# A planned linear-attention and feed-forward kernel: the order of units drawn anew, unread totals dropped, the last two copies in separate buffers

## Chip, cores and metric

The kernel runs on one core of a Trainium2 chip. The metric is device time in microseconds of one execution, the median of several. Before the change it is 183.63 us (four runs, 182.86 to 183.89).

## What is computed

Inputs are `q`, `k`, `v` and `f_logit`, each of shape (4 batches, 8 heads, 768 steps, 48), and two weights. A recurrent attention with a forget gate per key dimension comes first; its output, 3072 rows of 384, goes through a feed-forward block with exact GELU. All inputs and the output are float32.

```python
f = 1.0 / (1.0 + np.exp(-f_logit))
for t in range(S):
    state = f[:, :, t, :, None] * state + einsum('bhd,bhe->bhde', k[:, :, t], v[:, :, t])
    y[:, :, t] = einsum('bhd,bhde->bhe', q[:, :, t], state)
x = y.transpose(0, 2, 1, 3).reshape(3072, 384)
h = x @ w_in                                   # 384 -> 2048
out = (0.5 * h * (1 + erf(h / sqrt(2)))) @ w_out   # 2048 -> 384
```

## The kernel before, in words

**Chunks and units.** The 768 steps of a batch are cut into 6 chunks of 128, so there are 24 chunks n = 0..23, and two neighbouring chunks make a unit u = 0..11 (chunks 2u and 2u+1). Units 0 to 4 (`PAIRS`) hold their 256 steps interleaved ("pair" units, function `attn_pair`); units 5 to 11 hold the chunks one after the other (`attn_nat`). A unit is also a group g = u of the feed-forward block (`ffn_group`).

**Steps of a unit**, by the names that the plan gives them:

- `E`, `L` (ScalarE, L478 and L481): exponential and logarithm of the gate logits, in the table of exponentials.
- `C` (TensorE, L494 to L504): running sums of the log gates within a chunk, by a matmul with a triangle. Beside them, 4 small matmuls (8 for a pair unit, in its second half) compute the chunk's totals, into the same PSUM bank.
- `RG`, `GT`, `GL` (ScalarE, L509 to L518): exponentials of the negative sums, the sums and the totals.
- `KP`, `QP` (VectorE, L524): the keys and queries times these. `VC` (L529): the values in bf16, mostly on GpSimd.
- Transposes of both: by TensorE (`Tk`, `Tq`, L557) and a copy (`KQ`), or from unit 4 on by a DMA transpose (`KD`, L545).
- `S` (TensorE, L684 or L745): the chunk's addition to the state. `R` (VectorE) and `T`, `SB` (GpSimd) carry the state on with the totals `gl`. Chunk 5 of each batch needs none of this, since no chunk follows it.
- `A` (TensorE, L661 or L723) and `AM` (VectorE, L570): scores and their mask; `Y` (or `YI`, `YX`): the output; `YB`: its copy in bf16.
- `XT` and `X`, or from unit 5 on the DMA transpose `XD` (L618): the output transposed, as the input of the feed-forward block.
- `F1` (TensorE, L801): 8 steps of 6 matmuls to a group, each into one PSUM bank; `GE` (ScalarE, L811): GELU of each, in the table of GELU; `F2` (L820): for each chunk 4 steps of 4 matmuls, all into one bank; `O` (L834, for the last chunk L827): the copy to SBUF; `st`: the store.

`F1.8.5` is step 5 of group 8, `F2.17.2` step 2 of chunk 17.

**The planner.** `Plan.add` records every step with an estimated duration, what it reads and writes, its buffers and a priority. `Plan.run` places the steps one at a time, by its own estimate of time, and among those that can start in the same twentieth of a microsecond it takes the one with the lowest priority number. The order in which steps are placed is the order in which each engine's instructions are emitted, and it also decides which buffer a step gets. On the chip each engine then works through its list in order and waits at a step until what it needs is there. Before placing, each priority gets random amounts: a first one for all steps from one seed, and a second one from the generator of the step's unit (`SEEDS`, one seed per unit), whose width depends on the seed:

```python
if SEEDS[k]:
    w = (0.5, 1.0, 3.0, 8.0)[SEEDS[k] % 4]
    o.prio += own[k].uniform(-w, w)
```

When a step of ScalarE needs the other table than the last one, a table load is emitted ahead of it (L865).

**PSUM.** Of 8 banks 4 (`s_fh`) serve F1 and F2 (and the first units), 4 (`s_m`) the attention.

**Loads.** `LOADS` is the list of loads in order: `f3` is the gate logits of unit 3, `u4` all four inputs of unit 4, `i` and `o` pieces of the two weights, which GpSimd's queue loads. SyncE's queue issues all other loads, the stores and the DMA transposes, in one order. Where the list changes from one queue to the other, a load waits until an earlier weight has landed.

**Warm-up.** In the first 30 us, where the plan leaves TensorE idle, matmuls on a tile `junk` are put in (L859).

Of the kernel before, what the change touches and what calls it, by code (L numbers as in the profile page):

```python
# [9 lines left out]
F32 = mybir.dt.float32  # L10
BF16 = mybir.dt.bfloat16
AF = mybir.ActivationFunctionType
ALU = mybir.AluOpType
# [11 lines left out]

SPREAD, SEED = (1.0, 97)

SEEDS = [0, 684, 383, 3363, 2427, 131, 74, 3619, 3555, 1021, 519, 3174]

EAGER = 0.0  # L30

# [50 lines left out]
class Plan:  # L82
# [30 lines left out]
    def run(self):  # L113
# [4 lines left out]
        for o in self.ops:  # L118
            if o.prio > -5:
                k = min(max(int(o.prio % 1000) // 20, 0), len(SEEDS) - 1)  # L120
                o.prio += rng.uniform(-SPREAD, SPREAD)
                if SEEDS[k]:
                    w = (0.5, 1.0, 3.0, 8.0)[SEEDS[k] % 4]
                    o.prio += own[k].uniform(-w, w)
        act, switched, mode = None, 0.0, 0
        port = {"DVE": (0.0, 0.0), "POOL": (0.0, 0.0)}
        for o in self.ops:
# [75 lines left out]

SIZES = [2, 2, 2, 2, 2, 2, 2, 2, 2, 2, 2, 2]
PAIRS = [0, 1, 2, 3, 4]
WIN = [1024, 512, 512]
# [13 lines left out]
KDMA = [4, 5, 6, 7, 8, 9, 10, 11]  # L222
AJ = [2, 3, 4, 5, 6, 7, 8, 10, 11]
NGT = 4
WARM = 30.0
LOADS = ['f0', 'k0', 'v0', 'q0', 'f1', 'v1', 'k1', 'q1', 'i0', 'k2', 'f2', 'v2', 'q2', 'i1', 'i2', 'i3', 'o0', 'o1', 'o3', 'f3', 'o2', 'k3', 'q3', 'u4', 'v3']
LOADS += [f"u{n}" for n in range(12) if f"u{n}" not in LOADS and f"c{2 * n}" not in LOADS and f"f{n}" not in LOADS]


@with_exitstack  # L230
def kernel(
# [29 lines left out]
    def slots(n, shape, dt, name):  # L261
        return Slots(n, [one.tile(shape, dt, name=f"{name}{i}") for i in range(n)])
# [21 lines left out]
    s_vb = slots(10, [C, HD], BF16, "vb")  # L284
    s_gt, s_rg = slots(3, [C, HD], F32, "gt"), slots(3, [C, HD], F32, "rg")
    s_gl = slots(6, [C, 2, P2], F32, "gl")
    s_kq = slots(3, [C, 2, P2, 2, C], BF16, "kq")
    s_am = slots(8, [C, P2, C], BF16, "am")
    s_rr, s_tn = slots(3, [C, P2, 2 * D], F32, "rr"), slots(3, [C, P2, 2 * D], F32, "tn")
# [51 lines left out]
    for i in range(3):  # L341
        P.add("DVE", 0.2, lambda i=i: nc.vector.memset(
            s_sb.tiles[i].rearrange("p a b -> p (a b)").bitcast(F32), 0.0), wr=[f"sbz{i}"], prio=-70)
    z_lf = [f"lfz{i}" for i in range(3)]
    z_sc = [f"scz{i}" for i in range(NQ)]
    z_sb = [f"sbz{i}" for i in range(3)]
# [104 lines left out]
    def decays(u):  # L451
# [16 lines left out]
        for a, b, lo, hi in parts:  # L468
# [7 lines left out]
            def expop(lo=lo, hi=hi):  # L476
# [4 lines left out]
            P.add("ACT", d, lambda view=view, lo=lo, hi=hi: nc.scalar.activation(lf.t()[:, :, lo:hi, 0:D], view(), AF.Ln, bias=1.0),  # L481
                  rd=[("e", u, i) for i in range(a, b + 1)] + z_lf, wr=[("lf", u, i) for i in range(a, b + 1)],
                  bufs=[fl, lf], table="exp", prio=pr, name=f"L{u}")
        gps = [(s_fh if u in EG else s_m).new() for _ in range(2)]
        for j, n in enumerate(ns):
            y = X[n]
            gt, rg = s_gt.new(), s_rg.new()
            y.update(sc=s_sc.new(), vb=s_vb.new())
            pr = 20 * u + 10 * j

            def cum(j=j, g=gps[j]):
                g = g.t()
                if not pair:
                    nc.tensor.matmul(g[:, 0:HD], trin, lf.t()[:, j, :, 0:D], start=True, stop=True)  # L494
                    for p in range(P2):
                        nc.tensor.matmul(g[:, HD + p:HD + p + 1], lf.t()[:, j, 2 * p:2 * p + 2, :], negcol,  # L496
                                         start=True, stop=True, skip_group_check=True)
                    return
                nc.tensor.matmul(g[:, 0:HD], trip[:, 0, :], lf.t()[:, 0, :, 0:D], start=True, stop=False)
                nc.tensor.matmul(g[:, 0:HD], trip[:, 1 - j, :], lf.t()[:, 1, :, 0:D], start=False, stop=True)  # L500
                if j:
                    for i in range(2):
                        for p in range(P2):
                            nc.tensor.matmul(g[:, HD + 2 * p:HD + 2 * p + 2], lf.t()[:, i, 2 * p:2 * p + 2, :], negp,  # L504
                                             start=False, stop=(i == 1), skip_group_check=True)
            P.add("PE", (0.54 if j else 0.33) if pair else 0.27, cum,
                  rd=([("lf", u, 0), ("lf", u, 1), "trip", "negp"] if pair else [("lf", u, j), "trin", "negcol"]), wr=[("g", n)],
                  bufs=[lf, gps[j], gt, rg, y["sc"], gl], prio=pr, opens=gps[j], name=f"C{n}")
            P.add("ACT", 0.40, lambda g=gps[j], rg=rg: nc.scalar.activation(rg.t(), g.t()[:, 0:HD], AF.Exp, scale=-1.0),  # L509
                  rd=[("g", n)], wr=[("rg", n)], bufs=[gps[j], rg], table="exp", prio=pr, name=f"RG{n}")  # L510
            P.add("ACT", 0.40, lambda g=gps[j], gt=gt: nc.scalar.activation(gt.t(), g.t()[:, 0:HD], AF.Exp),  # L511
                  rd=[("g", n)], wr=[("gt", n)], bufs=[gps[j], gt], table="exp", prio=pr + 1, name=f"GT{n}")
            if not pair:
                P.add("ACT", 0.19, lambda g=gps[j], j=j: nc.scalar.activation(
                    gl.t()[:, j, :], g.t()[:, HD:HD + P2], AF.Exp),
                    rd=[("g", n)], wr=[("gl", n)], bufs=[gl, gps[j]], table="exp", prio=pr + 2, name=f"GL{n}")
            elif j:
                P.add("ACT", 0.19, lambda g=gps[j]: nc.scalar.activation(  # L518
                    gl.t(), g.t()[:, HD:HD + 2 * P2].rearrange("a (p c) -> a c p", c=2), AF.Exp),
                    rd=[("g", n)], wr=[("gl", n - 1), ("gl", n)], bufs=[gl, gps[j]], table="exp", prio=pr + 2,  # L520
                    name=f"GL{n}")
            for w, nm, a, b, off in ((0, "kp", "kt", rg, 0), (1, "qp", "qt", gt, 1)):
                pl = n in (GKP, GQP)[w]
                P.add("POOL" if pl else "DVE", 0.80 if pl else 0.475, lambda w=w, a=a, b=b, y=y, j=j, pl=pl: (nc.gpsimd if pl else nc.vector).tensor_tensor(  # L524
                    y["sc"].t()[:, w, :, 0:D], half(u, x[a], j), b.t().rearrange("p (h d) -> p h d", h=H), ALU.mult),
                    rd=[("gt" if w else "rg", n), (a, n)] + z_sc, wr=[(nm, n)], bufs=[y["sc"], x[a], b], prio=pr + off,
                    port=True, name=f"{nm.upper()}{n}")
            hv = u in HVC
            P.add("ACT" if hv else "POOL", 0.40 if hv else 0.47, lambda y=y, j=j, hv=hv: (nc.scalar.copy if hv else nc.gpsimd.tensor_copy)(  # L529
                y["vb"].t().rearrange("p (h d) -> p h d", h=H), half(u, x["vt"], j)),  # L530
                rd=[("vt", n)], wr=[("vb", n)], bufs=[y["vb"], x["vt"]], prio=pr, name=f"VC{n}")
# [173 lines left out]
    def attn_pair(u):  # L705
# [52 lines left out]
        def intra():  # L758
            for hh in range(2):
                for p in range(P2):  # L760
                    h = 2 * p + hh
                    for jk in range(2):
                        for cc in range(2):
# [2 lines left out]
                                             vbs[jk].t()[r, D * h:D * h + D], start=(h == 0 and jk == 0),  # L766
                                             stop=(cc == 0 and osb is None and hh == 1 and p == P2 - 1 and jk == 1),
                                             skip_group_check=True)
        P.add("PE", 0.5, intra, mode=1, rd=[("am", u, a, b) for a in range(2) for b in range(2)] + [("vb", n) for n in ns],
              wr=[("yi", n) for n in ns] + ([("yp", n0)] if osb is None else []), bufs=yps + vbs + sum(ams, []) + [U[u]["yb"]],  # L770
              prio=pr + PRI["Y"], opens=yps[0], name=f"YI{u}")
        for cc, n in enumerate(ns):
            o = (osb, mid)[cc]
            if o is None:
                continue
            P.add("PE", 0.2, lambda cc=cc, o=o: interp(yps[cc], kq, cc, o),
                  mode=1, rd=[("yi", n), ("sb", n - 1, 0), ("sb", n - 1, 1)] + [("kq", m) for m in ns], wr=[("yp", n)],
                  bufs=[yps[cc], kq, o], prio=pr + PRI["Y"] + 10 * cc, name=f"YX{n}")
# [3 lines left out]
    def ffn_group(g):  # L782
# [31 lines left out]
        for s_ in range(s):  # L814
            op, osb = s_fh.new(), s_os.new()
            n = first[g] + s_
            for r in range(4):
                def f2(s_=s_, r=r, op=op):
                    for fo in range(4 * r, 4 * r + 4):
# [2 lines left out]
                P.add("PE", 0.65, f2, rd=[("gT", g, fo // pk) for fo in range(4 * r, 4 * r + 4)] + [f"wout{r}"],  # L822
                      wr=[("o", n)], bufs=[op, gT], prio=pr + PRI["F"] + s_, held=True, name=f"F2.{n}.{r}")
            if n == NCH - 1:
                for i, eng in enumerate(("ACT", "DVE")):
                    h = slice(i * d_model // 2, (i + 1) * d_model // 2)
                    P.add(eng, 0.27, lambda h=h, i=i, op=op, osb=osb: copier(not i)(osb.t()[:, h], op.t()[:, h]),  # L827
                          rd=[("o", n)], wr=[("os", n, i)], bufs=[op, osb], prio=pr - 1000, name=f"O{n}")
                    P.add("DMA", 0.3, lambda h=h, i=i, n=n, osb=osb: (nc.sync if i else nc.scalar).dma_start(
                        out=out[n * C:(n + 1) * C, h], in_=osb.t()[:, h]), rd=[("os", n, i)], bufs=[osb], prio=-5, lag=4.0,  # L830
                        name=f"st{n}")
                continue
            od = n in ODVE
            P.add("DVE" if od else "ACT", 0.475 if od else 0.40, lambda op=op, osb=osb, od=od: copier(not od)(osb.t(), op.t()[:, 0:d_model]),  # L834
                  rd=[("o", n)], wr=[("os", n)], bufs=[op, osb], prio=pr - 1000, name=f"O{n}")
            P.add("DMA", 0.6, lambda n=n, osb=osb: nc.sync.dma_start(out=out[n * C:(n + 1) * C, :], in_=osb.t()),
                  rd=[("os", n)], bufs=[osb], prio=-5, lag=4.0, name=f"st{n}")

    g = 0
    for u in range(NU):  # L840
# [58 lines left out]
```

## Time and profile before

| | before |
|---|---|
| median of 4 runs | 183.63 us (182.86 to 183.89) |
| the profiled execution: its time | 183.65 us |
| its span in the profile | 181.5 us |
| busy: TensorE, ScalarE, VectorE, GpSimd | 172.4, 126.3, 95.2, 52.6 us |
| table loads of ScalarE at L865 | 15, 1283 ns each |
| granted TensorE clock | full |

The profile is of one execution; its time is 2.15 us more than its span. "Busy" is the time in which at least one instruction of the engine was under way; matmuls overlap, so a busy TensorE can still have waited within a step. In the profile's names `ps` is any PSUM bank, `sc` the products KP and QP, `lf` the log gates, `gl` the exponentials of the totals, `osb` the tile from which an output is stored.

### The profile page before, as it was taken

The numbers are of one execution on the slowest core, as the hardware profiler recorded it, in microseconds if no ns is written. First come the engines' busy times: TensorE is split into PE (matmuls) and PEld (weight loads), VectorE is DVE, ScalarE is ACT, GpSimd is POOL, SyncE is SP. The second block draws the span as 40 slices with busy tenths as digits, with TensorE's granted clock in tenths as the row PEclk, the third lists the DMA queues.
The fourth block names the chain that finished last, engine by engine and source line by source line (L and its number), as shares of the span: only waits on it lengthen the run. The fifth ranks groups of instructions, "written<-read, shape, count | busy, mean of one in ns | idle before, by whom it ended". The sixth has DMA issues, their size and how long they took to land.

```text
span 181.5 us, 4908 instructions
## 1 busy us (share of the span) xinstructions
PE 172.4 (95%) x1991; PEld 131.7 (73%) x1991; DVE 95.2 (52%) x185; ACT 126.3 (70%) x215; POOL 52.6 (29%) x116
## 2 busy tenths in 40 slices
PE   7689799999999999999999999999999999999992
PEld 2356479866778977669679689966696966887960
DVE  4289730068888650689277770627785217171020
ACT  2775098982986899989957689787483697360900
POOL 7757860003224810150352014014353112100000
PEclk9999999999999999999999999999999999999999
DMA  5999999999999999999999989989999973702112
GB/s 143 261 261 230 262 182 209 205 230 271 273 191 223 173 209 182 203 170 207 204 203 217 171 165 233 179 167 152 215 222 125 202 134 84 208 4 43 43 51 79
DMA packets 106933, 32.61 MB, mean 180 GB/s; under 512 B 102048, under 2 KB 106016, under 8 KB 106912
## 3 DMA queue, kind: packets, MB, share of 16 engines
q1 hardware_dynamic: 104992, 29.07, 76.8%
q0 software_dynamic: 1776, 3.15, 9.7%
q8 instruction: 15, 0.25, 0.6%
q10 hardware_dynamic: 144, 0.10, 0.2%
q14 instruction: 6, 0.05, 0.1%
HBM read 25.17 MB, written 4.72 MB: 165 GB/s over the span
## 4 chain that ended last, share of the span: by engine, by line
PE 79%; DMA 8%; SPq 6%; ACT 2%; DVE 2%; issue 1%; DVEq 0%; ACTq 0%
PE ps L801 33%; PE ps L820 32%; DMA fl<-in_f_logit_dram 6%; SPq L433 6%; DMA xT<-yb 2%; PE ps L661 2%; PE ps L697 2%; PE ps L494 1%; PE ps L638 1%; PE ps L684 1%; PE ps L723 1%; PE ps L557 1%; PE ps L765 1%; PE ps L745 1%; PE ps L644 1%
## 5 line engine op out<-in xcount | busy, mean ns | idle before, releaser
L811 ACT ACTIVATE gT<-ps 128x512 bf16<-128x512 f32 x96 | 58.5, 668 | 23.3 <-PE ps L801 21.7
L801 PE MATMUL ps<-xT,win 128*128 128x256 bf16 x576 | 68.6, 273 | 1.1 <-DMA win<-in_moe_w_in_dram 0.8
L820 PE MATMUL ps<-wout,gT 128*128 128x384 bf16 x384 | 68.3, 326 | 0.0
L801 PEld LDWEIGHTS <-win 128*128 128x128 bf16 x576 | 61.3, 114 | 3.6 <-DMA win<-in_moe_w_in_dram 1.1
L820 PEld LDWEIGHTS <-gT 128*128 128x128 bf16 x384 | 35.8, 98 | 20.9
L524 DVE TENSOR_TENSOR sc<-kt,rg 128x384 bf16<-128x384 f32 x23 | 14.1, 617 | 28.6 <-ACT rg L509 28.4
L596 POOL TENSOR_TENSOR tn<-rr,gl 128x384 f32<-128x384 f32 x16 | 13.9, 869 | 40.9 <-DVE rr L594 21.1
L529 POOL CAST vb<-vt 128x384 bf16<-128x384 f32 x22 | 12.0, 556 | 45.1 <-DMA vt<-in_v_dram 44.9
L570 DVE TENSOR_TENSOR am<-ps,mask 128x512 bf16<-128x512 f32 x28 | 17.5, 684 | 12.3 <-PE ps L661 12.3
L834 DVE COPY osb<-ps 128x384 f32<-128x384 f32 x20 | 11.1, 555 | 23.7 <-PE ps L820 17.6
L865 ACT ACT_TABLE_LOAD x15 | 19.2, 1283 | 0.3
L601 POOL CAST sb<-tn 48x192 bf16<-48x192 f32 x40 | 14.6, 364 | 13.4 <-DVE tn L590 7.8
L614 DVE CAST yb<-ps 128x384 bf16<-128x384 f32 x22 | 12.0, 555 | 8.3 <-PE ps L697 4.2
L509 ACT ACTIVATE rg<-ps 128x384 f32<-128x384 f32 x24 | 12.0, 502 | 5.3 <-PE ps L496 4.6
L478 ACT ACTIVATE fl<-fl 128x768 f32<-128x768 f32 x12 | 10.3, 855 | 7.4 <-DMA fl<-in_f_logit_dram 7.3
L511 ACT ACTIVATE gt<-ps 128x384 f32<-128x384 f32 x24 | 11.8, 500 | 5.1 <-PE ps L504 3.2
L570 DVE TENSOR_TENSOR am<-ps,maskp 128x512 bf16<-128x512 f32 x20 | 12.5, 684 | 2.7 <-PE ps L723 2.6
L524 DVE TENSOR_TENSOR sc<-qt,gt 128x384 bf16<-128x384 f32 x23 | 13.0, 571 | 1.2 <-ACT gt L511 0.9
L859 PE MATMUL ps<-junk 128*128 128x512 bf16 (+2 forms) x35 | 9.9, 413 | 1.5 <-POOL junk L851 1.3
L481 ACT ACTIVATE lf<-fl 128x768 bf16<-128x768 f32 x12 | 10.1, 845 | 0.4
L594 DVE TENSOR_TENSOR rr<-ps,tn 128x384 f32<-128x384 f32 x16 | 8.8, 553 | 1.4 <-POOL tn L596 0.5
L859 PEld LDWEIGHTS <-junk 128*128 128x128 bf16 x35 | 3.4, 109 | 5.3 <-issue 2.5
(68 smaller groups left out, 125.4 us busy)
## 6 DMA issues: line engine op xcount, KB each, us to landing
out_dram<-osb SPq DMA_DIRECT2D x23, 192.0 KB, 2.3
fl<-in_f_logit_dram SPq DMA_DIRECT2D x14, 192.0 KB, 3.8
kt<-in_k_dram SPq DMA_DIRECT2D x14, 192.0 KB, 4.0
qt<-in_q_dram SPq DMA_DIRECT2D x14, 192.0 KB, 4.0
vt<-in_v_dram SPq DMA_DIRECT2D x14, 192.0 KB, 3.6
fl<-in_f_logit_dram SPq DMA_DIRECT2D x5, 384.0 KB, 6.3
kt<-in_k_dram SPq DMA_DIRECT2D x5, 384.0 KB, 6.3
vt<-in_v_dram SPq DMA_DIRECT2D x5, 384.0 KB, 5.7
```

The lines of the kernel that those rows point to most:

```text
L509: P.add("ACT", 0.40, lambda g=gps[j], rg=rg: nc.scalar.activation(rg.t(), g.t()[:, 0:HD], AF.Exp, scale=-1.0), rd=[("g", n)], wr=[("rg", n ...
L524: P.add("POOL" if pl else "DVE", 0.80 if pl else 0.475, lambda w=w, a=a, b=b, y=y, j=j, pl=pl: (nc.gpsimd if pl else nc.vector).tensor_tensor(
L529: P.add("ACT" if hv else "POOL", 0.40 if hv else 0.47, lambda y=y, j=j, hv=hv: (nc.scalar.copy if hv else nc.gpsimd.tensor_copy)(y["vb"].t ...
L570: P.add("POOL" if pl else "DVE", 1.15 if pl else 0.61, lambda hh=hh, pl=pl: (nc.gpsimd if pl else nc.vector).tensor_tensor(ams[hh].t(), ap ...
L596: P.add("POOL", 0.83, lambda: nc.gpsimd.tensor_tensor(tn.t(), rr.t(), glb(), ALU.mult), rd=[("rr", n), ("gl", n)], wr=[("tn", n)], bufs=[r ...
L601: P.add("POOL", 0.36, lambda hh=hh: nc.gpsimd.tensor_copy(sb.t()[64 * hh:64 * hh + D, :, D * hh:D * hh + D], tn.t()[64 * hh:64 * hh + D, : ...
L614: P.add("ACT" if help_ else "DVE", 0.40 if help_ else 0.475, lambda: copier(help_)(yb.t()[:, i, :], yp.t()[:, 0:HD]), rd=[("yp", n)], wr=[ ...
L801: nc.tensor.matmul(hps.t()[:, i * tok:(i + 1) * tok].rearrange("a (s t) -> a s t", s=s), col(fo)[:, kk, :], xT.t()[:, :, kk, :], start=(kk ...
L811: nc.scalar.activation(to, fr, AF.Gelu)
L820: nc.tensor.matmul(op.t()[:, 0:d_model], gT.t()[:, fo, s_ * C:(s_ + 1) * C], wout[fo // 4][:, fo % 4, :], start=(fo == 0), stop=(fo == FO ...
L859: nc.tensor.matmul(o.opens.t()[:, 0:w], junk[:, 0:C], junk[:, 0:w], start=True, stop=True, skip_group_check=True)
L865: nc.scalar.preload_act_table_set({"exp": "natural_log_exp_and_others", "gelu": "gelu_and_others"}[o.table])
```

## The change

Five things change; a number of new switches that are left empty (`GLD`, `G1D`, `YJ`, `NUDGE`, `XA`) change nothing.

1. All twelve per-unit seeds are other numbers, so the priorities of all steps, and with them the order on every engine and the buffers, are drawn anew. Unit 0, which had no second draw, now has one.
2. The totals of a batch's last chunk are left out: for chunks 11, 17 and 23 the 4 small matmuls and the step `GL`; for chunk 5, in a pair unit, the matmuls have one column in place of two and `GL` writes half. As the unwritten half of `gl` would be undefined, 6 memsets on VectorE at the start set the tiles to 1.
3. The two halves of the last chunk's copy `O23` (ScalarE and VectorE) write two tiles in place of the halves of one.
4. The stores of chunks 16 to 19 are issued as two halves of 64 rows.
5. In the list of loads, `o2` (a piece of the second weight) stands ahead of `f3` in place of behind it. With it, `f3` waits for the landing of `o3` and no longer of `o1`.

ScalarE's program then has 17 table loads at this place in the code in place of 15, and chunk 22, not chunk 23, is the last whose F2 ends.

The step `GT` and the products are also written with other views of the same tiles; the order in memory and the shapes on the engines stay.

```diff
-SEEDS = [0, 684, 383, 3363, 2427, 131, 74, 3619, 3555, 1021, 519, 3174]
+SEEDS = [1643, 41, 995, 740, 2687, 1139, 2739, 2875, 1095, 1159, 531, 2848]
...
+ROWS = [16, 17, 18, 19]
...
-LOADS = [..., 'o0', 'o1', 'o3', 'f3', 'o2', 'k3', 'q3', 'u4', 'v3']
+LOADS = [..., 'o0', 'o1', 'o3', 'o2', 'f3', 'k3', 'q3', 'u4', 'v3']
...
+    for i in range(6):
+        P.add("DVE", 0.07, lambda i=i: nc.vector.memset(s_gl.tiles[i], 1.0), wr=[f"glz{i}"], prio=-60)
...
+        last = 2 * u + 1 if (2 * u + 1) % nC == nC - 1 else None
+            ends = 1 if last else 2
...
-                    for p in range(P2):
+                    for p in range(0 if gld or n == last else P2):
                         nc.tensor.matmul(g[:, HD + p:HD + p + 1], lf.t()[:, j, 2 * p:2 * p + 2, :], negcol,
                                          start=True, stop=True, skip_group_check=True)
...
             if n == NCH - 1:
+                osbs = (osb, s_os.new())
                 for i, eng in enumerate(("ACT", "DVE")):
...
-                    P.add(eng, 0.27, lambda h=h, i=i, op=op, osb=osb: copier(not i)(osb.t()[:, h], op.t()[:, h]),
-                          rd=[("o", n)], wr=[("os", n, i)], bufs=[op, osb], prio=pr - 1000, name=f"O{n}")
+                    P.add(eng, 0.27, lambda h=h, i=i, op=op, osb=osbs[i]: copier(not i)(osb.t()[:, h], op.t()[:, h]),
+                          rd=[("o", n)], wr=[("os", n, i)], bufs=[op, osbs[i]], prio=pr - 1000, name=f"O{n}")
...
+            def store(n=n, osb=osb):
+                w = C // 2 if n in ROWS else C
+                for r in range(0, C, w):
+                    nc.sync.dma_start(out=out[n * C + r:n * C + r + w, :], in_=osb.t()[r:r + w, :])
```

Of the order that the new priorities give, the places that matter below, on TensorE and ScalarE (`*` is a count of steps; before above, after below):

```
TensorE  ... A2 F2.0*2 C7 C6 ...             ... C12 C13 F2.7*2 S12 F2.7 ...
         ... F2.1*2 F2.0 A2 F2.0 F2.2 C6 C7  ... C12 C13 F2.7*2 F1.4 S12 F1.4 ...
TensorE  F1.7*8 between:  A17 F1.7*3 Y16 F1.7 Y17 F1.7 F2.12 F2.13*4 F2.12 C18 C19 F2.12*2 S18
                          F1.7.7 F1.7.4 A17 F2.12*3 C18 Y16 C19 Y17 F1.7.0 F2.13*3 F2.12 F2.13 S18
ScalarE  GE5*8 E8 L8 GT16 RG16 GL16 GT17 GL17 RG17 GE6*8 GE7*8 E9 L9 RG18 ...
         GE5*8 GE6*6 E8 L8 RG16 GL16 GT16 GT17 RG17 GE6*2 GE7*5 E9 L9 GE7*3 RG18 ...
VectorE  ... AM19*2 YB19 R21 ...
         ... AM19*2 KP21 R20 YB19 QP21 R21 ...
TensorE, the end:  F1.11*8 F2.21 F2.22*4 F2.23*4
                   F1.11*8 F2.22 F2.23 F2.22 F2.23*3 F2.22*2
```

## The prediction

> **What bounds the kernel now.** First the page: busy times and the chain that ended last.
>
> ```profile
> PE 172.4 (95%) x1991; PEld 131.7 (73%) x1991; DVE 95.2 (52%) x185; ACT 126.3 (70%) x215; POOL 52.6 (29%) x116
> ...
> PE 79%; DMA 8%; SPq 6%; ACT 2%; DVE 2%; issue 1%; DVEq 0%; ACTq 0%
> ```
>
> TensorE is busy for 95% of the span and is 79% of the chain, so an order can only win what TensorE still waits for, what it need not compute, and what lies before and behind its work. Next the timeline of ScalarE, for when the dense work begins:
>
> ```profile
> 22.61 0.84 ACT L478 ACTIVATE fl<-fl 128x768 f32<-128x768 f32 x1 [4.09 <-DMA fl<-in_f_logit_dram]
> ...
> 24.36 1.28 ACT L865 ACT_TABLE_LOAD   x1
> 25.65 3.13 ACT L811 ACTIVATE gT<-ps 128x512 bf16<-128x512 f32 x5
> ```
>
> The third load of gate logits lands at 22.6; E2, L2, a table load and the first GELU follow, which frees a bank; F1.1 starts at 27.09, and from then on TensorE hardly stops. Its waits, in total, from the list of waits (the longer ones there are of the start):
>
> ```profile
> PE ps L801 <- DMA xT<-yb: 0.3, 1, 0.3
> PE ps L723 <- DVE kq L563: 0.3, 1, 0.3
> ...
> PE ps L684 <- DVE sc L524: 0.2, 1, 0.2
> ```
>
> These are lower bounds, as matmuls overlap. So I took each step's distance to the next step's start from TensorE's timeline. From 27.09 to the end of the last matmul, 177.91, are 150.82 us: 92 steps F1 at 0.655 (60.26), 96 steps F2 at 0.650 (62.40), the attention at its usual distances 24.97, together 147.63; 17 entries from full-height matmuls into those on 64 rows (A, S, YI of pair units), 0.096 each, 1.63; the last matmul running out 0.16; four waits, 0.20 (A2), 0.34 (S12), 0.08 (S15) and 0.43 (F1.9.2), 1.05; small differences 0.35. The sum is 150.82. The time behind it: last matmul 177.91, last landing 180.31, span 181.5, time 183.65. The profiled time stands 0.02 over the median of 183.63.
>
> **The change part by part.** *Start.* The orders of SyncE's and GpSimd's queues up to fl2 are the same, so 22.6 stays. GT0 now goes ahead of RG0, which puts KP0 back by 0.38 (7.23 against 6.84), but QP0 waits until 9.07 for the landing of q anyway. The 6 memsets take VectorE some 0.14 each, 0.84, in its 4.34 us of idle before 7.37; without that cover they would cost 0.84. Nothing, then. `f3` is issued when o3 lands (36.28) instead of o1 (34.42). By k3, which went at 36.30 and took 4.55, it lands at 40.9; by the median of such loads, 6.3, at 42.6. E3 and L3 (1.74) and 0.15 for the hand-over bring C6's earliest start to 42.8 or 44.5; TensorE comes to C6 at 44.3. I take the first, as f3 replaces k3 in the same place: nothing; at worst 0.2. The loads behind move back by one place, about 1.3; fl4, now in the place of k4 (39.39, landing 45.78), is there before E4's turn on ScalarE at 46.3.
>
> *Totals.* 3 chunks lose 4 matmuls: C takes 0.262 with them and 0.17 (the triangle alone, 0.16 to 0.18) without, so 3 x 0.09 = 0.27 less on TensorE. Three GL (0.17 to 0.25) go from ScalarE, hidden.
>
> *Order: what goes.* One of 17 entries into the 64-row steps goes: 0.10. A2's wait goes: behind Tq5 stand three F2 (1.95) in place of one (0.65), over two KQ copies of 0.65. S12's place:
>
> ```profile
> 77.34 0.33 PE L494 MATMUL ps<-lf,trin 128*128 128x384 bf16 x1
> ...
> 77.87 1.46 PE L820 MATMUL ps<-wout,gT 128*128 128x384 bf16 x8
> 79.50 0.34 PE L684 MATMUL ps<-vb,sc 128*128 128x96 bf16 x4 [0.17 <-DVE sc L524]
> ```
>
> From C12 to S12 are 2.16; the product between them took 1.14 instead of 0.55, beside work of GpSimd:
>
> ```profile
> 78.30 1.14 DVE L524 TENSOR_TENSOR sc<-kt,rg 128x384 bf16<-128x384 f32 x1 [0.21 <-ACT rg L509]
> ```
>
> The new order has two F2 and an F1 there, with the C 2.48, so no wait even so. S15 gets four steps of cover: none. F1.9.2 waits for XD19, the transposed output of unit 9. Its cover from Y19 is the same 4.73 (S21 0.17, three F1, and before three F2 with A21 0.65, now four F2), and YB19 now stands behind KP21 and R20 on VectorE (1.0 more), though YB19 would have to wait for Y19 for most of that; in SyncE's queue XD19 is now ahead of KD21. Transposes landed 2.7 to 4.6 after issue, this one 4.08. I keep 0.30, between 0 and 0.9.
>
> *Order: what comes.* ScalarE has 17 table loads at L865's place in place of 15. What a switch costs the chain:
>
> ```profile
> 99.40 0.60 ACT L811 ACTIVATE gT<-ps 128x512 bf16<-128x512 f32 x1 [0.44 <-PE ps L801]
> 100.01 1.28 ACT L865 ACT_TABLE_LOAD   x1
> 101.31 0.84 ACT L478 ACTIVATE fl<-fl 128x768 f32<-128x768 f32 x1
> 102.19 0.84 ACT L481 ACTIVATE lf<-fl 128x768 bf16<-128x768 f32 x1
> ```
>
> The GELU starts 0.21 behind the end of its F1 (98.53 + 0.655), the load 0.61 later, E 1.30 after that, L 0.88 after that and ends after 0.84: 3.84 from F1's end, 3.95 with the hand-over to C. Over this TensorE has, in the new order: before C16 two Y, four F2, one F1: 4.00, no wait. Before C18 two F1, A17 with its entry, three F2: 3.91, wait 0.05. Then S18, which is new: between E9, L9 and RG18 now stand GELU 7.7, 7.4 and 7.0 with a load on either side. From the end of F1.7.1: 3.84, load 1.30, three GELU at 0.58 (nine took 5.18 from 109.31) 1.74, load 1.30, RG 0.52, KP 0.56, hand-over 0.10: 9.36. TensorE's work there: two F1 1.31, A17 0.65, three F2 1.95, C18, Y16, C19, Y17 1.28, F1.7.0 0.655, five F2 3.25: 9.10. Wait 0.26.
>
> The Trainium skill, "ScalarE: Activation LUTs", section "What ACT_TABLE_LOAD costs", speaks against the added switches: to the 1283 ns of the load it adds a drain of about 1380 ns, 2.66 us a switch. The trace has the load and 0.02 us, so I go by the trace; by the page S18, with two switches on its way, would wait 2.8 us longer.
>
> The other new waits: F2.4.0 wants GELU 2.1, whose F1 ends 0.99 earlier (XT6, XT7, one F1), against 0.21 + 0.76 + hand-over 0.10: 0.08. It also keeps one of four banks from then until chunk 4 is copied, while E5 and L5 with two loads split the GELUs of group 3: F1.3.3 has 5.87 of TensorE's work behind F1.3.6 (three F1, three F2, YI4, YX8, YX9, two XT, C10, C11) to cover GELU 3.6, load, E5, L5, load and GELU 3.4, 6.05: 0.2. Sum of the waits that come or stay: 0.30 + 0.05 + 0.26 + 0.08 + 0.20 = 0.89, against 1.05.
>
> *End.*
>
> ```profile
> 177.94 0.32 ACT L827 COPY osb<-ps 128x192 f32<-128x192 f32 x1 [5.25 <-PE ps L820]
> 178.29 0.37 ACTq L829 DMA_DIRECT2D out_dram<-osb  x1
> 178.30 0.36 DVE L827 COPY osb<-ps 128x192 f32<-128x192 f32 x1 [2.34 <-ACT osb L827]
> 178.68 0.33 SPq L829 DMA_DIRECT2D out_dram<-osb  x1
> ```
>
> The two copies went one after the other; in separate tiles the second would start 0.36 sooner. But the chunk that ends last is now 22: one copy of 0.56 on VectorE and one store of 192 KB. The three such stores before took 1.85 from issue to landing, the two half stores 1.69 and 1.63. From the last matmul: 0.04 + 0.56 + 0.02 + 1.85 = 2.47, against 2.40 before: 0.07 more. Had chunk 23 ended last, 0.36 less. The four split stores add four issues of about 0.35 to SyncE at 140 to 156, behind them XD21 and KD22, which landed at 147.9 and 155.6, 7.5 and 2.6 before F1.10.0 and A23: nothing.
>
> Sum: -0.27 - 0.10 - 1.05 + 0.89 + 0.07 = -0.46; 183.65 - 0.46 = 183.19, say 183.2.
>
> **The rivals.** *ScalarE too late (slower).* In the stretch from GE5's end to RG18 (100.0 to 122.8 before) the new list has five table loads in place of three: 2.6 more, over idle times that sum to 4.2 there. My sum needs these to fall where they help. C16 has a margin of 0.05, C18 and S18 none: from there every 0.1 of delay on ScalarE or in the product KP18 (0.55 alone, 1.18 beside GpSimd) is 0.1 of time. One load uncovered gives 183.2 + 1.3 = 184.5, both 185.8. For it: TensorE's cover is equal to the chain within 0.3 in three places. Against it: before, C22 followed an equal chain with 3.9 of cover and did not wait.
>
> *All waits vanish (faster).* The order is drawn so that none of my small waits is real: -0.27 - 0.10 - 1.05 + 0.07 = -1.35, 182.3. No order can do better as long as the start is the same. Against it: S18's sum and XD19.
>
> *The load queue (slower, small).* One transfer later from 36 us on: if fl4 went another place later and landed as q4 did (47.20), E4, L4 and the hand-over would end at 49.1, where TensorE comes to C8 at 48.8: 0.3 more, 183.5. It lies in the forecast's range.
>
> **How the numbers follow.** A measurement of this kernel can tell about 0.5%, 0.92 us, from no change. The forecast, small waits traded for small waits, holds 182.7 to 184.5, own point 183.2: 0.57. Waits nearly gone: 0.18. ScalarE too late, or an unseen wait of that size: 0.25. The range for 8 in 10 reaches from the floor, 182.3, to a little over one uncovered load, 185.0.
>
> **What would show it.** Right: F1.1 starts near 27.1, the last matmul ends near 177.5, the last store is of 128x384 and lands 2.5 later; S18 waits for KP18 by 0.2 to 0.3; A2 and S12 do not wait. Wrong: a wait of TensorE over 0.6 at C16, C18 or S18; a GELU that frees its bank late in group 3; C6 waiting for L3; or a start that moved, since I took it as fixed by the third load of logits.

## The result, and the profile after

The kernel after takes 184.10 us in the median of 44 runs (183.32 to 186.72); on the same chips the kernel before takes 183.56 us (63 runs, 182.86 to 184.87). The ratio is 1.003, 95% interval 1.0017 to 1.0042: slower by about half a microsecond, where 0.46 us less was forecast. The profiled execution took 184.12 us, its span is 182.0 us.

The page of the kernel after, busy times and the chain that ended last:

```profile
PE 173.0 (95%) x1978; PEld 131.9 (72%) x1978; DVE 95.9 (53%) x191; ACT 129.3 (71%) x214; POOL 53.2 (29%) x116
...
PE 70%; DMA 16%; SPq 6%; ACT 3%; issue 1%; DVE 1%; DVEq 0%; ACTq 0%
```

DMA has doubled its share of the chain, from 8% to 16%. The list of TensorE's waits (us in total, times, longest) says where, in the lines that are not of the start:

```profile
PE ps L713 <- DMA kq<-sc: 0.9, 3, 0.4
...
PE ps L866 <- DMA xT<-yb: 0.5, 1, 0.5
...
PE ps L866 <- ACT gT L876: 0.2, 1, 0.2
```

`kq<-sc` is the DMA transpose of keys and queries (KD), `xT<-yb` that of the attention's output (XD). The first of these lines is new and the second has grown from 0.3; both are waits for transposes, and the change edits no transpose, only their places in the order. The third is one wait for a GELU to free a bank.

With distances between the starts of steps, as in the prediction: F1.1 starts at 26.98 (27.09 before), and from there to the end of the last matmul, 178.61, are 151.63 us against 150.82, so +0.81. The start gives 0.11 back, the end takes 0.08 (2.48 against 2.40), and 0.28 less lies behind the last landing: +0.50 of span. The waits of this stretch, 1.05 before, are 2.43: F1.5.7 for XD11 0.64; in A17 for KD17 0.36; A18 for KD18 0.43; in A21 for KD21 0.47; F1.3.3 for its bank 0.33; F2.16.1 for a GELU 0.20. The four transposes make 1.90. Two of these waits in TensorE's timeline, F1.5.7 and the second half of A17:

```profile
92.16 0.81 PE L866 MATMUL ps<-xT,win 128*128 128x256 bf16 x6 [0.48 <-DMA xT<-yb]
...
116.75 0.40 PE L713 MATMUL ps<-kq 64*128 64x128 bf16 x8 [0.18 <-DMA kq<-sc]
```

**Why four transposes are late.** SyncE's part of the timeline, the two KD that A18 and A19 need and the one that A21 needs:

```profile
125.63 2.78 SPq L597 DMA_TRANSPOSE kq<-sc  x2
...
137.75 1.25 SPq L597 DMA_TRANSPOSE kq<-sc  x1
```

TensorE's part at the same places, A18 and the second half of A21:

```profile
130.56 0.40 PE L713 MATMUL ps<-kq 64*128 64x128 bf16 x8 [0.39 <-DMA kq<-sc]
...
142.70 0.40 PE L713 MATMUL ps<-kq 64*128 64x128 bf16 x8 [0.30 <-DMA kq<-sc]
```

KD18's issue ended at 126.86 and it landed at 130.52, 3.65 later; KD21's ended at 139.00, landing 142.65, also 3.65. KD20 in between, issue ended 134.59, took 2.17. What differs is a row that I passed over in the page's list of DMA queues (packets, MB, share of 16 engines):

```profile
q8 instruction: 15, 0.25, 0.6%
```

Fifteen packets of 16 KB (and some smaller ones on another queue). Their number fits a fetch of TensorE's own program, one for every 256 of its 3956 matmuls and weight loads, and the experiments below move them by adding such instructions. In the dense part one comes about every 12 us, each 0.9 to 1.3 us long. In the kernel after those from 85 to 145 us began at 89.25, 102.03, 114.06, 128.24 and 140.65. The DMA view of the stretch from 128.0 to 132.0, busy tenths and traffic in 40 slices of 0.1 us:

```profile
DMA  9993899999990000100000799999999998999854
GB/s 212 261 242 67 174 197 212 207 189 179 90 33 0 0 3 8 10 10 8 10 10 10 156 287 289 287 321 420 430 369 415 384 338 246 338 338 323 265 96 94
```

The packet begins in the third slice; 0.9 us later the traffic of all 16 engines falls from about 200 GB/s to 10 or less and stays there for 1.0 us. KD18 lands when it is over. Behind the fetch at 140.65, which KD21 met, there is no such standstill. This is the stretch from 140.2 to 144.2:

```profile
DMA  9533944798999999999999652244668999999899
GB/s 162 101 58 77 244 67 90 154 157 157 200 228 223 225 229 223 232 238 234 202 204 217 133 102 56 54 92 100 125 127 157 175 198 240 229 209 186 173 190 192
```

Traffic falls to 54 GB/s at the lowest, and KD21 took as long as KD18. So a standstill is not the whole of it. The experiments below test whether the fetches make the transposes late; how they do it stays open.

### The profile page after: what moved, and what is told of

Its sections match the earlier page's. It is cut to its first block, busy times and chain, and to the rows that moved or that the text cites. A ratio compares the mean times of both kernels' runs of the same rounds, so it can differ in the third digit from the quotient of the medians.

```text
span 182.0 us, 4895 instructions
## 1 busy us (share of the span) xinstructions
PE 173.0 (95%) x1978; PEld 131.9 (72%) x1978; DVE 95.9 (53%) x191; ACT 129.3 (71%) x214; POOL 53.2 (29%) x116
## 4 chain that ended last, share of the span: by engine, by line
PE 70%; DMA 16%; SPq 6%; ACT 3%; issue 1%; DVE 1%; DVEq 0%; ACTq 0%
PE ps L866 31%; PE ps L885 27%; DMA kq<-sc 8%; DMA fl<-in_f_logit_dram 6%; SPq L447 6%; DMA xT<-yb 3%; PE ps L713 2%; ACT L934 1%; PE ps L749 1%; ACT gT L876 1%; PE ps L519 1%; PE ps L609 1%; PE ps L690 1%; PE ps L775 1%; PE ps L736 1%
## 5 line engine op out<-in xcount | busy, mean ns | idle before, releaser
L876 ACT ACTIVATE gT<-ps 128x512 bf16<-128x512 f32 x96 | 59.1, 667 | 21.9 <-PE ps L866 19.7
L866 PE MATMUL ps<-xT,win 128*128 128x256 bf16 x576 | 69.3, 273 | 1.1 <-DMA xT<-yb 0.5
L574 DVE TENSOR_TENSOR sc<-qt,gt 128x384 bf16<-128x384 f32 x23 | 14.1, 618 | 4.5 <-ACT gt L547 4.5
L928 PE MATMUL ps<-junk 128*128 128x512 bf16 (+3 forms) x34 | 10.5, 443 | 1.7 <-POOL junk L920 1.3
```

Source lines behind the costliest of these rows:

```text
L866: nc.tensor.matmul(hps.t()[:, i * tok:(i + 1) * tok].rearrange("a (s t) -> a s t", s=s), col(fo)[:, kk, :], xT.t()[:, :, kk, :], start=(kk ...
L876: nc.scalar.activation(to, fr, AF.Gelu)
L928: nc.tensor.matmul(o.opens.t()[:, 0:w], junk[:, 0:C], junk[:, 0:w], start=True, stop=True, skip_group_check=True)
```

## The experiments

Two theories. *Fetches*: a DMA transpose that is in flight while 16 KB of TensorE's program are fetched lands 1 to 2 us later; the new order and the 26 instructions fewer put fetches onto four transposes that have nothing to spare, while in the kernel before they fell on three (KD10, KD11, XD13) with 0.3 to 2.4 us to spare, and on the last part of two more (XD11, KD21), which were not late. *Order* (the rival): the new places of the transposes in SyncE's queue make them late, whatever is fetched. The fetches can be moved alone: some wide matmuls on `junk` of the warm-up are exchanged for many of two columns, which were meant to take about the same time together but are more instructions.

**First four: the fetches moved from the start.** The edit, with 88, 140 and 56 small matmuls in the kernel after and 64 in the kernel before (88 is shown):

```diff
+EXTRA = 88
...
+                if o.name == "C0":
+                    for _ in range(EXTRA):
+                        nc.tensor.matmul(o.opens.t()[:, 0:2], junk[:, 0:C], junk[:, 0:2], start=True, stop=True, skip_group_check=True)
+                    room -= EXTRA // 3
```

*After, +160 instructions.* 

> The changed kernel with 160 more instructions in TensorE's program ahead of the first step (88 matmuls of 2 columns on the junk tile, 8 wide junk matmuls fewer); all else as in the changed kernel. Theory (fetch): TensorE's program is fetched in pieces of 16 KB, 256 instructions each, and a DMA transpose that is under way during a fetch lands 0.8 to 1.7 us later; in the changed kernel this hits XD11, KD17, KD18 and KD21, for which TensorE waits 0.64, 0.36, 0.43 and 0.47 us. 160 instructions earlier, the fetches fall on KD12 and XD13, which have 3.3 and 2.4 us to spare. So these four waits go, S18 waits 0.2 to 0.3 as its cover shrinks, and the time is 182.2 to 182.8. Rival (queue order): the transposes are late because of the loads and stores beside them in SyncE's queue; then the same four land as late as before and the time is 184.0 to 184.3. Either way the first F1.1 starts within 0.3 us of 27.0.

*After, +256, one whole period.* 

> The changed kernel with 256 more instructions in TensorE's program ahead of the first step (140 matmuls of 2 columns, 12 wide junk matmuls fewer), a whole piece of 256, so that the fetches fall where they fell. Fetch theory: transposes XD11, KD17, KD18 and KD21 are hit as in the changed kernel, time 183.9 to 184.3. Queue order: the same time. If it is the added matmuls as such that help (or harm), this run shows it: then it goes the way of the run with 160 more.

*After, +102.* 

> The changed kernel with 102 more instructions in TensorE's program ahead of the first step (56 matmuls of 2 columns, 5 wide ones fewer). Fetch theory: the fetches now fall on KD13 (0.7 us to spare), KD14 or KD15 (1.1), XD15 and KD20 (3 and 5); so XD11, KD17, KD18 and KD21 are no longer late, but A13 waits 0.5 to 0.9 us for KD13 and A15 up to 0.4 for KD15: 183.0 to 183.6. Queue order: no change, 184.0 to 184.3.

*Before, +116.* 

> The kernel before the change with 116 more instructions in TensorE's program ahead of the first step (64 matmuls of 2 columns, 6 wide ones fewer). Fetch theory: before, the fetches fall on KD10, KD11, XD13 and on the queue between KD21 and XD19; now on KD13 (9 us to spare) and at most KD16 and KD20 (over 2). A2 (0.20) and S12 (0.34) still wait; F1.9.2 waits 0 to 0.2 in place of 0.43 for XD19: 183.1 to 183.5. Queue order: no change, 183.5 to 183.7.

Measured on one chip, where the kernel before took 183.69 us (26 runs); the ratio is not simply that of the two medians:

| kernel | us, median | ratio to before (95%) | F1.1 starts | F1.1 to last matmul | waits of TensorE for XD11, KD17, KD18, KD21 |
|---|---|---|---|---|---|
| after +102 | 182.99 | 0.9953 (0.9919 to 0.9988) | 27.26 | 150.26 | 0, 0, 0.44, 0 |
| after +160 | 183.45 | 0.9999 (0.9976 to 1.0022) | 28.85 | 150.61 | 0, 0, 0, 0 |
| after +256 | 185.01 | 1.0080 (1.0048 to 1.0112) | 27.98 | 151.91 | 0.96, 0.17, 0.57, 0.48 |
| before +116 | 183.35 | 0.9983 (0.9970 to 0.9997) | 27.14 | 150.50 | (F1.9.2 for XD19: 0, was 0.43) |

The waits on the transposes with a whole period (first two lines) and with 102 (last line):

```profile
PE ps L714 <- DMA kq<-sc: 0.8, 2, 0.5
PE ps L867 <- DMA xT<-yb: 0.8, 1, 0.8
```

```profile
PE ps L714 <- DMA kq<-sc: 0.4, 1, 0.4
```

Nothing was moved in any queue, yet all four waits go with 160, three of them with 102, and all four return with a whole period. The transposes follow the fetches: from the end of the issue to landing KD17 took 3.48 in the kernel after and 3.29 with a whole period, where it met a fetch, and 1.90 and 1.85 with 160 and 102, where it met none; KD21 took 3.65 and 3.65, against 1.95 and 2.29. The rival falls for XD11, KD17 and KD21. For KD18 it keeps something: with 102, no fetch met KD18 (2.07 from the end of the issue to landing), but it was issued at 126.32, behind a load whose issue SyncE held from 124.99 to 126.21, and A18 still waited 0.44.

Missed in my expectations: with 102, A13 did not wait, since KD13 landed only 0.40 behind the start of the fetch (1.98 from the end of its issue), and A15 did not although a fetch met KD15 (2.88); and the additional matmuls at C0 were not neutral, since with 160 and 256 F1.1 started 1.9 and 1.0 later. With 160 also S21 waited 0.79, for the cast of its values. Their load met the fetch at 132.85, the longest of all with 1.94 us, and took 4.48 from the end of its issue to landing, where the same load took 2.58 to 3.44 in the other nine profiles. So a fetch can also make an ordinary load late.

**The parts without the new order.** The kernel before, its order kept, with the totals of chunks 11, 17 and 23 left out and the last copies in separate tiles. `TINY` exchanges one wide matmul on `junk` ahead of F1.1.0 for eight small ones, so that the count of instructions stays about the same; its code is shown with the next kernel:

```diff
+TINY = {'F1.1.0': (1, 8)}
...
-                    for p in range(P2):
+                    for p in range(0 if (2 * u + j) % nC == nC - 1 else P2):
...
-                P.add("ACT", 0.19, lambda g=gps[j], j=j: nc.scalar.activation(
+                P.add("ACT", 0.19, lambda g=gps[j], j=j, n=n: None if n % nC == nC - 1 else nc.scalar.activation(
...
+                osbs = (osb, s_os.new())
-                    P.add(eng, 0.27, lambda h=h, i=i, op=op, osb=osb: copier(not i)(osb.t()[:, h], op.t()[:, h]),
+                    P.add(eng, 0.27, lambda h=h, i=i, op=op, osb=osbs[i]: copier(not i)(osb.t()[:, h], op.t()[:, h]),
```

> Kernel before with its order kept; taken over from the change are only the totals of the last chunk of each batch, left out (12 matmuls and 3 exponentials less, none of them read by anything), and the last two half copies, now in separate tiles. One wide matmul on junk ahead of F1.1.0 is replaced by eight of two columns, so that the count of TensorE's instructions behind it, and with it the places where its program is fetched, stays about as in the kernel before. By the prediction's steps: 0.27 less for the totals and, as chunk 23 ends last here, 0.36 less for the copies: 183.0. If two engines that copy halves of one bank of PSUM take turns even with separate targets: 0.27 less, the two copies still 0.03 apart, 183.3. If the transposes' landings hang on the fetches: nothing more, waits as before (A2 0.2, S12 0.3, F1.9.2 0.4).

Measured: 183.47 us, ratio 0.9995 (0.997 to 1.002) against 183.52 for the kernel before on this chip (31 runs), which the next three comparisons use too. The 0.27 is too small for this interval, so inconclusive for the totals. It is clear for the copies, the end of its timeline:

```profile
178.81 0.32 ACT L829 COPY osb<-ps 128x192 f32<-128x192 f32 x1 [5.25 <-PE ps L821]
179.16 0.37 ACTq L831 DMA_DIRECT2D out_dram<-osb  x1
179.17 0.36 DVE L829 COPY osb<-ps 128x192 f32<-128x192 f32 x1 [2.34 <-ACT osb L829]
```

VectorE starts 0.04 behind ScalarE's end, as with one tile: the separate tiles win nothing, and the 0.36 that I had for them is not there. The fetches were not held in place as intended: the one at 136.75 in the kernel before came at 137.57, met KD21 on its way, and in this order too TensorE waited for it, longer than at any place of the kernel after:

```profile
138.32 0.40 PE L662 MATMUL ps<-kq 64*128 64x128 bf16 x8
139.62 0.40 PE L662 MATMUL ps<-kq 64*128 64x128 bf16 x8 [0.90 <-DMA kq<-sc]
```

KD21's issue ended at 135.95, landing 139.57, 3.62; in the kernel before 135.46 and 137.23, 1.77. A18 waited too, by 0.41 in the list, although no fetch came between the end of KD18's issue and its landing (1.99): the issue itself took 2.55, as in the kernel before, and a fetch at 125.01 fell into it. That wait is not one that the theory counts, and its cause was not tested. This profiled execution took 184.48, the others 182.56 to 184.41.

**The kernel before, +50.** Three wide matmuls on `junk` ahead of F1.1.0 against 28 small ones:

```diff
+TINY = {'F1.1.0': (3, 28)}
...
+                drop, tiny = TINY.get(o.name, (0, 0))
+                room -= 4 * drop
+                for _ in range(tiny):
+                    nc.tensor.matmul(o.opens.t()[:, 0:2], junk[:, 0:C], junk[:, 0:2], start=True, stop=True, skip_group_check=True)
```

> Kernel before, order kept; three wide matmuls on junk ahead of F1.1.0 are replaced by 28 of two columns (50 instructions more on TensorE from there on, the same time within 0.1). Theory of the fetches: the fetches move some 2 to 3 us ahead and now meet KD17, KD20 and KD21, of which KD20 and KD21 have 0.6 us to spare or less; they land 1 to 1.7 later, A21 waits 0.6 to 1.0, time 184.0 to 184.5 though no step has moved. Theory of the order (the places of transposes in the queues set the waits): the same queues, so the same waits as before, 183.6.

Measured: 183.61 us, ratio 1.0018 (0.9996 to 1.0039). The fetches at 112.12 and 136.21 met KD17 (3.53) and KD21 (3.34), as expected, and not KD20; but KD21, issued 0.35 earlier, landed at 138.44, and A21 waited only 0.09 for it. So the landings moved as the theory says and the time hardly did: a miss of mine by some 0.5 us, since a meeting costs only what it exceeds the margin by.

**The kernel after, +104 behind the start.** The same exchange in three later places, so that the loads of the start are not disturbed:

```diff
+TINY = {'A1.1': (3, 20), 'F1.0.1': (3, 20), 'F1.1.3': (3, 21)}
```

> Kernel after, order kept; in A1.1, F1.0.1 and F1.1.3 nine wide matmuls on junk are replaced by 61 of two columns (104 instructions more, put behind the loads of the start). Theory of the fetches: as with the 102 instructions at C0, the fetches miss XD11, KD17, KD18 and KD21; from F1.1 to the last matmul 150.3, F1.1 at 27.0, so 182.7, with F1.3.3 0.33 and A18 0.4 left. Theory of the order: XD11 0.64, KD17 0.36, KD18 0.43 and KD21 0.47 stay, 184.1.

Measured: 182.69 us, ratio to before 0.9942 (0.9915 to 0.9969): the version that beats both kernels, the one before by 0.83 us (on this chip) and the one after by 1.4 us (against its 184.10 above). F1.1 starts at 26.89, from there to the last matmul 150.49. Its chain, and the only wait for a transfer in the list of TensorE's waits (0.8 of it lies in the start, as before):

```profile
PE 83%; DMA 7%; DVE 3%; ACT 3%; POOL 1%; issue 1%; DVEq 0%; POOLq 0%
```

```profile
PE ps L867 <- DMA win<-in_moe_w_in_dram: 1.2, 2, 0.8
```

No wait for a transpose is left in the list (by distances, A13 waits 0.13 for KD13). A18 does not wait either (I expected 0.4): KD18 was issued 0.54 earlier than with 102 at C0. In its place F1.0.6 waits 0.35 for a piece of the first weight (0.51 by distances).

**The same with two loads put behind KD18 and KD19.**

```diff
+    for name in ("qt10.1", "kt10.1"):
+        o = next(x for x in P.placed if x.name == name)
+        P.placed.remove(o)
+        P.placed.insert(1 + max(i for i, x in enumerate(P.placed) if x.name == "KD19"), o)
```

> The kernel with the 104 instructions behind the start, and with the two loads of q and k of the last unit but one (units of pairs, 10.1) moved behind KD18 and KD19 in SyncE's queue. If the 0.44 that A18 still waits with fetches out of the way is the queue's (KD18 is issued behind a load that waits for its buffer, 1.3 late): that wait goes, 182.3. If KD18 is late for another reason: 182.7 as without the move. The later loads could make S21 or KP21 wait: they have some 8 us to spare.

Measured: 183.05 us, ratio 0.9967 (0.9949 to 0.9985), not the 182.3 hoped for. KD18 landed 1.43 earlier (128.02 against 129.45), as the queue's order would have it, but nothing waited for it any more. The load of v behind the moved ones was issued at 130.58 in place of 129.83 and landed at 134.41 in place of 132.90, and S21 waited for its cast:

```profile
134.54 0.50 POOL L582 CAST vb<-vt 128x384 bf16<-128x384 f32 x1 [5.51 <-DMA vt<-in_v_dram]
...
135.09 0.33 PE L737 MATMUL ps<-vb,sc 128*128 128x96 bf16 x4 [0.42 <-POOL vb L582]
```

My expectation weighed the two moved loads and not the one queued behind them.

**All ten profiles together.** Each has 23 DMA transposes. Of the 230, 180 had no fetch of more than 0.8 us between the end of the issue and the landing: they took 1.20 to 2.50 us. Of the 50 that had one, 41 took 2.60 to 4.04. The other nine took 1.77 to 2.11: they landed within 0.84 us of the start of the fetch, while none of the 41 landed sooner than 1.96 us after it. No transpose without a fetch took as long as any of the 41. This is a count over whatever the kernels put side by side; that the fetch is the cause is shown by the kernels in which it alone was moved.

## Why the prediction was wrong, step by step

*Right.* The start did not move (26.98 for 27.09); C6 did not wait for the later `f3`. The chunks without totals: C takes 0.16 in place of 0.26. The waits of A2, S12, S15 and F1.9.2 are gone, as reckoned or better: XD19 landed at 139.61, 1.0 before its use, where I had kept 0.30. S12's place in the kernel after, with the F1 in between and no wait:

```profile
77.55 1.46 PE L885 MATMUL ps<-wout,gT 128*128 128x384 bf16 x8
78.84 0.82 PE L866 MATMUL ps<-xT,win 128*128 128x256 bf16 x6
79.50 0.33 PE L736 MATMUL ps<-vb,sc 128*128 128x96 bf16 x4
```

The tail, reckoned at 2.47, took 2.48, with chunk 22 last; its two lines:

```profile
178.65 0.56 DVE L900 COPY osb<-ps 128x384 f32<-128x384 f32 x1 [0.59 <-PE ps L885]
179.23 0.33 SPq L905 DMA_DIRECT2D out_dram<-osb  x1
```

*Mis-sized, small.* The entry into 64-row steps that was to go (0.10) did not: by the shapes of the matmuls there are 16 from F1.1 on before, not 17, and 16 after; 13 of these now follow an F1 or F2, the others Tk4, C21 and Y18. F1.3.3 waited 0.33 (0.20 in the sum). S18 (0.26), C18 (0.05) and F2.4.0 (0.08) did not wait. ScalarE's list over S18's chain came as drawn:

```profile
115.58 1.28 ACT L934 ACT_TABLE_LOAD   x1
...
118.61 1.28 ACT L934 ACT_TABLE_LOAD   x1
...
121.79 1.28 ACT L934 ACT_TABLE_LOAD   x1
123.08 0.49 ACT L541 ACTIVATE rg<-ps 128x384 f32<-128x384 f32 x1
```

A17's wait of 0.36 stands inside TensorE's side of that sum and gave ScalarE the time; with the wait gone, in the kernels with +102 and +104, S18 waited 0.06 by distances, so 0.26 was too much by 0.2. F2.16.1's 0.20 for a GELU was not seen. The separate tiles of the last copies were taken to start the second 0.36 sooner; it still starts behind the first.

*The step that failed* is the one called "what comes": the sum of the waits that come or stay, 0.89. It is worked out from the order of steps and the engines' durations. The only transposes whose landing the prediction weighs are XD19, XD21 and KD22. The other twenty, A17's, A18's, A21's and F1.5.7's among them, were given no term, and they cost 1.90. The row that would have warned stood in the prediction: "transposes landed 2.7 to 4.6 after issue". I took that as scatter and took bounds from it for one transpose. It is the range of the seven XD from the start of the issue, and two things are mixed in it. The longest, XD13, had met a fetch: it took 3.41 from the end of its issue, where the other six took 1.51 to 2.17. The next, XD19, had met none; its issue alone took 2.52.

*The sum again with this term.* The prediction has 150.29 for the stretch from F1.1 to the last matmul (150.82 - 0.27 - 0.10 - 1.05 + 0.89). Take away the waits that did not come (0.30, 0.26, 0.05, 0.08), add 0.13 for F1.3.3, 0.20 for F2.16.1 and 1.90 for the transposes: 151.83, measured 151.63. With +102, the 1.90 is 0.44: 150.37, measured 150.26. With +104 it is nothing, but 0.51 for F1.0.6 and 0.13 for A13's transpose: 150.57, measured 150.49. The accounting of the order holds within 0.2 us in three kernels (within 0.3 if the 0.10 for the entry is put back); what it lacked was where the program's own fetches fall.

*The rivals.* ScalarE too late: no, C16, C18 and S18 did not wait. The load queue: no, C8 did not wait. All waits vanish: no. The 0.25 for "slower" had an unseen wait in it without a place. The time came out inside the band of 182.7 to 184.5 that had the chance of 0.57, but that band stood for small waits traded for small waits: that it held is luck, since waits of 1.90 that the sum did not have were partly made up by waits that did not come.

## What to carry to other kernels

An instruction list is also a transfer. When transposes or loads come just in time, put the times of the instruction fetches beside them before a new order is judged, and try the same order with the fetches moved by a third or a half of their period: here that moved the time by 1.4 us, the change as a whole by 0.5 us. And when the durations of one kind of transfer fall into two clumps, find out what makes the second one before using the mean or the ends.

## What the runs showed of the hardware

**Around a fetch of 16 KB the other transfers can stand nearly still for about a microsecond.** In the ten profiles, between 45 and 146 us, traffic averages about 196 GB/s. In slices of 0.1 us, it stayed below 20 GB/s for at least half a microsecond 46 times, and 43 of these standstills began within 3 us of the start of a 16 KB fetch, where chance would put little over a quarter of them. I had not expected that of a single packet. It is not the rule, though: of the 96 fetches in these stretches 43 were followed by a standstill, 25 of the 40 that met a transpose and 18 of the other 56. Why the engines pause is open; no run separates the transpose in flight from the loads queued behind it.

The Trainium skill, "Runtime: NRT & Kernel Launch", section "Instruction fetch mechanics", has the block of 16 KB and 256 instructions, which the packets in the trace fit; it calls the cost of crossing a block mostly hidden. For TensorE itself that agrees, as no wait for the fetch appears in its list. Of other transfers under way the section says nothing; here 41 transposes took 2.60 to 4.04 us in place of 1.20 to 2.50.

**More instructions at C0 also moved the start.** With 160 and 256 more a fetch came at 6.74 and 6.29, the second load of gate logits landed 1.3 and 1.0 later (11.82 and 11.46 for 10.51), and F1.1 began at 28.85 and 27.98 in place of 26.98. That the fetch is the cause there was not tested by itself.

**Two engines that read halves of one bank of PSUM** came one after the other in all the kernels, VectorE 0.03 to 0.04 us behind ScalarE, with separate targets too. In the traces VectorE's copy waits for a semaphore that ScalarE's copy updates. The Trainium skill, "PSUM — Partial Sum Buffer", section "PSUM bank collisions raise a hardware error", gives a reason for such a wait: two engines must not touch one bank on the same partitions at once, reads against reads included. I had not weighed that rule in the prediction. The runs agree as far as the order of the copies goes; a version without the wait was not tried.
